# One buffer each for rounded q and its remainder, 24 resident weight tiles, and k's subtraction halved in one block of six, in a fused attention and soft-MoE kernel

## The chip, the cores and the metric

The kernel runs on one core of one Trainium2 chip. The metric is device time in microseconds (us) of one execution.

## The reference

```python
scores = scale * np.matmul(q, k.transpose(0, 1, 3, 2))   # 8 batches, 12 heads, 448 x 64
scores = np.where(causal mask, -1e9, scores)
attn = softmax(scores)
x = (attn @ v) reordered to (3584, 768)                   # rows: tokens, columns: heads
logits = x @ phi                                          # 768 x 32 slots
d = softmax of logits over all 3584 tokens; slot_input = d.T @ x
slot_out[e] = relu(slot_input[e] @ w1[e]) @ w2[e]         # 8 experts, 4 slots each, 768 -> 1024 -> 768
c = softmax of logits over the slots
return c @ slot_out
```

All arrays are float32. The weights w1 and w2 of the eight experts are 50.3 MB together, read once.

## The kernel before, in words

**Two parts.** The first part (about 300 us) is attention, with the logits and slot sums kept up to date behind it. The second (about 100 us) runs the experts and writes the output. The weights come as 64 tiles of 768 KB (`[128, 1536]` f32). `RES` of them are resident: they have a place of their own and are loaded during attention, one every other block. The next `TW1` tiles lie where the buffers of attention lay, so each of their loads waits until the last reader of the buffer under it is done; the rest reuse places of tiles that are used up. `place` and `slot` (lines 144 to 161) say which.

**Attention by pairs.** `block(p)` (lines 536 to 650) runs for each of 48 pairs of heads; pair p has heads a = 2p and a + 1. The engines take their instructions in the order in which the program is written; all of them are recorded by one helper, so every row of the profile has line 65, and one goes by tile names. q and k are split into a rounded value and a remainder, so that the fast matmul gives float32 scores:

- `cast_q`, `cast_k` (ACT, lines 226 to 232) round the raw q into `qd`, the raw k into `ks`. In the profile: `qd<-qk` and `ks<-qk`.
- `sub_k` (POOL, line 234) replaces the lower 64 partitions of `ks` by raw k minus rounded k: `ks<-qk,ks`. `sub_q` (POOL, line 244) writes raw q minus rounded q to the lower half of `r2`: `r<-qk,qd`. One instruction does both heads (64x896), or one head (64x448).
- `copy_k2` (ACT) copies rounded k into `k2`: `k<-ks`.
- `scores1` (PE, line 250) is the first pass, `ks` by `qd`, with the mask: `s<-qd,ks`, `s<-tri,identb`. Its first product of a head, part "k3", takes the last 64 rows of the head and two columns more (`KP`, line 265): the profile shows a weight load of 66 columns. For the first head of a pair those two columns belong to the second head.
- `max_keys`, `max_row` (DVE, PE) find a maximum for every block of 32 queries, giving `mr`. `max_spread` (POOL, line 315) writes it into the upper rows of `r2`: `r<-mr`, called a spread below.
- `scores2` (PE, line 326) is the second pass, `k2` by `r2`: `s<-r,k`. It adds the remainder of q and takes off the maximum. `exps` (ACT) is the exponential, `pt<-s`; `attv_pair` (PE) is `po<-va,pt`; `xtrans` (PE) is `xm<-ident,x`.

Block p finishes pair p (second pass, exponentials, attention times v), does the first pass of pair p + 1, the subtractions `sub_q(p + 1)` and `sub_k(p + 2)`, the casts `cast_q(p + 2)` and `cast_k(p + 3)`, and issues the loads of raw q of pair p + 3 and raw k of pair p + 4 on SP's queue, each behind the subtraction that frees its buffer. `qd`, `r2` and `ks` have two buffers each (`NR = 2`, lines 100 to 108), taken in turn by pairs; the raw values share four (`raw`, line 92).

POOL's work in a block is, in order: `sub_q`, `sub_k`, the spread of head a + 2, the spread of head a + 3. One block in six (p % 6 == 2, p over 6: p = 8, 14, 20, 26, 32, 38, 44) has the softmax step of the logits of a batch as well (`logits_b`, `logits_d`, `logits_e`). Below, "the block of the logits" is such a block, and the text uses p = 32, between 207 and 214 us.

**The start.** `warm(n)` (line 214) puts n matmuls without use on PE, to keep it running; `START` says how many at which place. Pairs 0 and 1 are done head by head.

Of the kernel before, what the change touches and what calls it, by code (L numbers as in the profile page):

```python
# [17 lines left out]
P = 128  # L18
# [7 lines left out]
NCH = 4  # L26
# [4 lines left out]
NEG = -float(2 ** 33)  # L31
NHD = 2 * NPAIR
NR, XB, XT = 2, 3, 2
RES, TW1 = 23, 12

HT = 2
WN, PAD = 1536, 168
WARM = (2, 5, 2, 3, 3)
START = (8, 3, 2)


FILL = 9
# [38 lines left out]
def attention_soft_moe(ctx: ExitStack, tc: tile.TileContext, qk, va, phi, w1, w2, out):  # L81
    nc = _Core(tc)
    const = ctx.enter_context(tc.tile_pool(name="const", bufs=1, side="left"))
    wone = ctx.enter_context(tc.tile_pool(name="wone", bufs=1, side="left"))
# [7 lines left out]
    raw = early.enter_context(tc.tile_pool(name="raw", bufs=4, side="right"))  # L92
# [4 lines left out]


    x_, va_, pt_ = [None] * XB, [None, None], [None, None]
    qd_, ks_ = [fix.tile([P, 2, S], F32R, name="qd0")], [fix.tile([P, 2 * S + KP], F32R, name="ks0")]  # L100
    r2_ = [fix.tile([P, 2, S], F32R, name="r20")]
    qd_.append(fix.tile([P, 2, S], F32R, name="qd1"))
    ks_.append(fix.tile([P, 2 * S + KP], F32R, name="ks1"))
    va_[0] = fix.tile([P, NCH, 2, VC], F32, name="va0")
    x_[1] = fix.tile([P, NCH, 3 * P], F32, name="x1")
    r_ = [fix.tile([P, RW], F32, name=f"r{i}") for i in range(2)]
    k2_ = fix.tile([P, 2 * S + KP], F32R, name="k2")
    r2_.append(fix.tile([P, 2, S], F32R, name="r21"))
    pt_[0] = wk.tile([P, 1024], F32, name="pt0")
    va_[1] = wk.tile([P, NCH, 2, VC], F32, name="va1")  # L110
    pt_[1] = wk.tile([P, 1024], F32, name="pt1")
    ltn = moe.tile([P, P + 1], F32, name="lt")
    lt = ltn[:, 0:P]

    x_[2] = moe.tile([P, NCH, 3 * P], F32, name="x2")
    x_[0] = moe.tile([P, NCH, 3 * P], F32, name="x0")
    gs = moe.tile([P, P], F32, name="gs")
    mk = moe.tile([P, P], F32, name="mk")

    st = {}  # L120

    def load_qk(p, a, hs=slice(0, 2), eng=nc.sync):
        if p < NPAIR:
            if hs.start == 0:

                st["raw", a, p] = (wres.tile([P, 2 * WN], F32, tag="w", name=f"qk{a}_{p}")[:, 0:2 * S]
                                   .rearrange("p (h s) -> p h s", h=2)
                                   if (p, a) in ((1, 0), (2, 1)) else
                                   raw.tile([P, 2, S], F32, tag="qk", name=f"qk{a}_{p}"))
            eng.dma_start(out=st["raw", a, p][:, hs], in_=qk[p, :, a, hs])  # L130

    def loads_v(p, eng=nc.sync):
# [18 lines left out]
    def slot(n, name, dtype=F32):  # L151
        m = place(n)
        if m >= RES:
            return wt[0].tile([P, WN], dtype, tag=f"wa{m}", name=name)
        if m == RES - 1:
            return wone.tile([P, WN], dtype, tag="w1", name=name)
# [41 lines left out]
    for x in (x_[1], x_[0], x_[2]):  # L198
        nc.vector.memset(x[:, NCH - 1], 0.0)
    nc.scalar.activation(out=identb, in_=ident, func=AF.Copy)  # L200
    load_qk(1, 1, eng=nc.scalar)
    load_qk(2, 0)
    load_qk(3, 1)
    for i in range(NR):
        nc.gpsimd.memset(r2_[i][0:64, :, :].bitcast(F32), 0.0)
# [19 lines left out]

    def cast_q(p, hs=slice(0, 2)):
        if p < NPAIR:
            nc.scalar.activation(out=qd_[p % NR][:, hs], in_=st["raw", 0, p][:, hs], func=AF.Copy)

    def cast_k(p, hs=slice(0, 2)):  # L230
        if p < NPAIR:
# [11 lines left out]

    def sub_q(p, hs=slice(0, 2), eng=None):
        if p < NPAIR:
            (eng or nc.gpsimd).tensor_tensor(out=r2_[p % NR][64:P, hs], in0=st["raw", 0, p][64:P, hs],
                                             in1=qd_[p % NR][64:P, hs], op=ALU.subtract)


    def scores1(i, part):  # L250
        if i >= NHD:
            return
        p, h = divmod(i, 2)
        ks, qd = ks_[p % NR], qd_[p % NR]
# [60 lines left out]
    def max_spread(i):  # L315
        if i >= NHD:
            return
        p, h = divmod(i, 2)
        mr = st.pop(("mr", i))

        nc.gpsimd.affine_select(out=r2_[p % NR][0:NQB, h].rearrange("p (b t)->p b t", t=32),
                                in_=mr.unsqueeze(1).to_broadcast([NQB, NQB, 32]),
                                compare_op=ALU.is_equal, fill=0.0, base=0,
                                pattern=[[-1, NQB], [0, 32]], channel_multiplier=1)

    def scores2(i, cs):
        if i >= NHD:
            return
        p, h = divmod(i, 2)
        s = st["s", i]  # L330
        k2, r2 = k2_, r2_[p % NR]
# [187 lines left out]
    cast_k(0, h1)  # L519
    cast_q(0, h1)  # L520
    sub_k(0, h1)
    max_row(0, 0)
    max_row(0, 1)
    max_spread(0)
# [11 lines left out]
    def block(p):  # L536
        a, b = 2 * p, p // 6 - 1
        last, m6 = p == NPAIR - 1, p % 6
        if p + 1 < NPAIR:
            loads_v(p + 1, nc.sync if p + 1 < NPAIR - 1 else nc.scalar)  # L540
        if p % 2 and p // 2 < RES - 1 or p == 2 * RES - 2:
            load_w(p // 2)

        if last:
            for f in last_of:
# [5 lines left out]
        if p == 0:  # L551
            copy_k2(0, h1)
            cast_q(1, h1)
            max_row(1, 0)
# [55 lines left out]
        max_row(a + 2, 1)  # L610
        max_spread(a + 2)
        if p == 0:
            sub_q(1, h1)
            load_qk(3, 0)
        for k in (1, 2):
            max_keys(a + 3, k)
        for k in range(2):
# [350 lines left out]
```

## Time and profile before

| what | value |
|---|---|
| median of 3 runs | 404.52 us (403.7 to 406.21) |
| the profiled execution, device time | 403.89 us |
| its span in the trace | 402.2 us |
| busy: PE, PEld, DVE, ACT, POOL | 368.3, 295.8, 293.7, 282.4, 265.3 us |
| DMA | 119.17 MB, 294 GB/s over the span |
| granted TensorE clock | 0.984 |

In a timeline row the columns are the start, the time of the group, engine, line, operation, written tile <- read tiles, their shapes and the count; in brackets stands the idle time of the engine before it and what ended it. PEld is TensorE's weight load, which runs beside PE. A row of the stretches gives the length, busy time and number of instructions of each engine, the granted clock, the busy share of the DMA engines and what they moved.

### The profile page before, as it was taken

How to read it: one execution, taken by the hardware profiler on the slowest of the kernel's cores; microseconds unless marked ns; L12 is line 12 of the kernel's file. 1: busy time of each engine (PE TensorE's matmuls, PEld its weight loads, DVE VectorE, ACT ScalarE, POOL GpSimd, SP SyncE). 2: the span in 40 equal slices, each digit the busy share in tenths (PEclk: the TensorE clock that was granted, in tenths of full speed). 3: DMA queues.
4: the chain of work that ended last, by engine and by line, in shares of the span. 5: the costliest groups of instructions: out<-in, count | busy, mean ns of one | idle time of the engine just before them, and what ended most of it. 6: DMA issues, size and time to landing. Idle time of an engine off the chain costs nothing.

```text
span 402.2 us, 14066 instructions
## 1 busy us (share of the span) xinstructions
PE 368.3 (92%) x5756; PEld 295.8 (74%) x5756; DVE 293.7 (73%) x834; ACT 282.4 (70%) x395; POOL 265.3 (66%) x214
## 2 busy tenths in 40 slices
PE   6889899999999999999999999999999989997840
PEld 3678888898988898888888889888876544542420
DVE  5868788788898888898888888888975575342540
ACT  5878798898898888888888988988952112432430
POOL 5899899898898988898988989888950000000000
PEclk9999999999999999999999999999999999999985
DMA  8668877878787788777788787788679999999997
GB/s 304 230 199 282 271 266 228 245 279 278 229 286 262 244 269 289 256 240 265 262 270 259 249 272 238 274 286 257 216 279 415 420 420 423 424 418 413 398 397 339
DMA packets 34480, 119.17 MB, mean 296 GB/s; under 512 B 3824, under 2 KB 8944, under 8 KB 32880
## 3 DMA queue, kind: packets, MB, share of 16 engines
q1 hardware_dynamic: 34128, 117.55, 82.2%
q8 instruction: 45, 0.74, 0.7%
q10 hardware_dynamic: 288, 0.73, 0.5%
q14 instruction: 19, 0.16, 0.1%
HBM read 107.25 MB, written 11.01 MB: 294 GB/s over the span
## 4 chain that ended last, share of the span: by engine, by line
PE 54%; DMA 16%; POOL 12%; issue 5%; ACT 4%; DVE 4%; SPq 1%; POOLq 0%; DVEq 0%; ACTq 0%
PE s L65 28%; PE po L65 17%; DMA w<-in_w_dram 14%; POOL r L65 7%; POOL ks L65 5%; PE xm L65 3%; PE rt L65 1%; ACT ks L65 1%; PE pp L65 1%; DVE r L65 1%; DMA qk<-in_qk_dram 1%; PE hp L65 1%; ACT k L65 1%; DVE si L65 1%; PE e L65 1%
## 5 line engine op out<-in xcount | busy, mean ns | idle before, releaser
L65 DVE TRANSPOSE_TENSOR_REDUCE r<-s 128x32 f32<-128x1024 f32 x96 | 119.5, 1245 | 11.4 <-PE s L65 9.3
L65 ACT ACTIVATE pt<-s 128x1024 f32<-128x1024 f32 x96 | 98.8, 1029 | 40.6 <-PE s L65 37.8
L65 PEld LDWEIGHTS po<-va,pt 128*64 128x64 f32 x3040 | 103.6, 138 | 12.0 <-issue 11.9
L65 PE MATMUL po<-va,pt 128*64 128x65 f32 x3040 | 110.6, 224 | 0.0
L65 POOL TENSOR_TENSOR r<-qk,qd 64x896 fp32r<-64x896 f32 (+1 forms) x50 | 101.7, 2033 | 5.5 <-ACT qd L65 1.8
L65 POOL TENSOR_TENSOR ks<-qk,ks 64x896 fp32r<-64x896 f32 (+1 forms) x49 | 99.2, 2024 | 0.2
L65 PE MATMUL s<-qd,ks 128*128 128x448 f32 (+4 forms) x384 | 80.8, 322 | 0.6 <-POOL ks L65 0.4
L65 POOL TENSOR_SCALAR_AFFINE_SELECT r<-mr 14x448 fp32r<-14x448 f32 x96 | 61.5, 643 | 29.8 <-PE xm L65 18.6
L65 PE MATMUL s<-r,k 128*128 128x448 f32 (+3 forms) x384 | 65.2, 292 | 5.0 <-POOL r L65 4.3
L65 PEld LDWEIGHTS s<-r,k 128*128 128x128 f32 (+1 forms) x384 | 59.3, 176 | 11.0 <-POOL r L65 8.8
L65 PEld LDWEIGHTS s<-qd,ks 128*128 128x128 f32 (+2 forms) x384 | 52.8, 184 | 3.7 <-issue 1.4
L65 ACT ACTIVATE qd<-qk 128x896 fp32r<-128x896 f32 (+1 forms) x50 | 46.0, 920 | 1.7 <-DMA qk<-in_qk_dram 0.8
L65 ACT ACTIVATE k<-ks 64x896 fp32r<-64x896 f32 (+1 forms) x49 | 45.8, 934 | 1.2
L65 ACT ACTIVATE ks<-qk 128x896 fp32r<-128x896 f32 (+1 forms) x51 | 45.4, 892 | 1.1 <-DMA qk<-in_qk_dram 1.0
L65 PE MATMUL s<-tri,identb 128*128 128x192 bf16 x192 | 39.4, 270 | 1.1 <-DVE si L65 0.4
L65 DVE TENSOR_REDUCE r<-r 128x16 f32<-128x32 f32 x192 | 33.7, 176 | 5.0
L65 DVE TENSOR_REDUCE mr<-s 14x32 f32<-14x128 f32 x47 | 13.1, 279 | 23.1 <-ACT ks L65 12.8
L65 PE MATMUL xm<-ident,x 128*128 128x128 f32 x188 | 28.3, 273 | 0.0
L65 ACT ACTIVATE xts<-xm 128x512 f32<-128x512 f32 x47 | 27.8, 592 | 0.2 <-PE xm L65 0.2
L65 DVE TENSOR_SCALAR x<-po,sm 64x64 f32<-64x64 f32 x94 | 25.9, 276 | 0.7
L65 DVE TENSOR_TENSOR x<-po,sm 128x384 f32<-128x384 f32 (+2 forms) x49 | 25.7, 526 | 0.0
L65 DVE COPY ot<-pp 128x384 f32<-128x384 f32 x26 | 13.6, 554 | 13.4 <-PE pp L65 13.3
(138 smaller groups left out, 391.0 us busy)
## 6 DMA issues: line engine op xcount, KB each, us to landing
qk<-in_qk_dram SPq DMA_DIRECT2D x93, 448.0 KB, 4.4
w<-in_w_dram SPq DMA_DIRECT2D x43, 768.0 KB, 7.0
w<-in_w_dram SPq DMA_DIRECT2D x10, 1536.0 KB, 21.0
va<-in_va_dram SPq DMA_DIRECT2D x47, 260.0 KB, 4.6
out_dram<-ot SPq DMA_DIRECT2D x16, 384.0 KB, 6.7
out_dram<-ot SPq DMA_DIRECT2D x2, 1536.0 KB, 9.2
qk<-in_qk_dram SPq DMA_DIRECT2D x4, 224.0 KB, 3.9
hw<-in_w_dram SPq DMA_DIRECT2D x1, 768.0 KB, 8.4
```

Of the source, the lines that this page charges most:

```text
L65: return self._tc.keep_in_program_order(op(*args, **kwargs))
```

## The change

It has five parts.

1. `qd` and `r2` get one buffer each. So `cast_q(p + 2)` in block p has to follow `sub_q(p + 1)`, which reads `qd`; and `sub_q(p + 1)` has to follow the second passes of pair p, which read `r2`.
2. In a block, `sub_k(p + 2)` now stands ahead of `sub_q(p + 1)`, and `cast_k(p + 3)` ahead of `cast_q(p + 2)`. The loads behind them change places in the same way. Raw k and raw q have two buffers each instead of four together.
3. In the block of the logits, and in block 1, `sub_k` is halved: the first head's half stands ahead of `sub_q`, the second head's half behind both spreads, and the load of raw k of pair p + 4 behind that.
4. `RES` goes from 23 to 24 and `TW1` from 12 to 11. Two more blocks (16 and 30) load a tile, block 44 none. All resident tiles now lie in pairs. The buffers of attention are placed in another order, which changes which reader a later load waits for.
5. At the start, raw k of pair 1 is loaded by SP instead of ACT's queue, behind the loads of pair 0; raw k of pair 3 is loaded after `sub_k(0)`; the subtractions of pairs 1 to 3 stand in another order; one of two memsets of `r2` goes; `START` is (9, 6, 2, 4) in place of (8, 3, 2): one, three and four more warming matmuls, the last group at a new place.

The diff without the renaming of buffers:

```diff
-RES, TW1 = 23, 12
+RES, TW1 = 24, 11
-START = (8, 3, 2)
+START = (9, 6, 2, 4)
...
-    qd_, ks_ = [fix.tile([P, 2, S], F32R, name="qd0")], [fix.tile([P, 2 * S + KP], F32R, name="ks0")]
-    r2_ = [fix.tile([P, 2, S], F32R, name="r20")]
-    qd_.append(fix.tile([P, 2, S], F32R, name="qd1"))
+    kraw = {n: fix.tile([P, 2, S], F32, name=f"kraw{n}") for n in (0, 1)}
+    qraw = {0: fix.tile([P, 2, S], F32, name="qraw0")}
+    ks_ = [fix.tile([P, 2 * S + KP], F32R, name="ks0")]
+    qd = fix.tile([P, 2, S], F32R, name="qd")
     ks_.append(fix.tile([P, 2 * S + KP], F32R, name="ks1"))
+    qraw[1] = fix.tile([P, 2, S], F32, name="qraw1")
...
-    r2_.append(fix.tile([P, 2, S], F32R, name="r21"))
+    r2 = fix.tile([P, 2, S], F32R, name="r2")
...
-            if n <= NBUF or q >= RES - 1:
+            if n <= NBUF or q >= RES:
...
     for hs in (slice(0, 1), slice(1, 2)):
         load_qk(0, 1, hs)
         load_qk(0, 0, hs)
+    load_qk(1, 1)
     load_qk(1, 0)
...
-    load_qk(1, 1, eng=nc.scalar)
     load_qk(2, 0)
-    load_qk(3, 1)
+    nc.gpsimd.memset(r2[0:64, :, :].bitcast(F32), 0.0)
...
-        if p % 2 and p // 2 < RES - 1 or p == 2 * RES - 2:
-            load_w(p // 2)
+        if p % 2 and p < 44 or p in (16, 30):
+            load_w(st["w"])
+            st["w"] += 1
...
-        if p:
+        late_k = p == 1 or m6 == 2 and p > 6
+        if p == 1:
+            sub_q(2, h0)
+            sub_k(3, h0)
+            sub_q(2, h1)
+            load_qk(4, 0)
+        elif p:
+            sub_k(p + 2, h0 if late_k else slice(0, 2))
+            if not late_k:
+                load_qk(p + 4, 1)
             sub_q(p + 1)
             load_qk(p + 3, 0)
-            sub_k(p + 2)
-            load_qk(p + 4, 1)
         else:
             sub_q(1, h0)
+            sub_q(1, h1)
+            load_qk(3, 0)
             sub_k(2, h0)
...
-        cast_q(p + 2)
-        cast_k(p + 3)
+        if p:
+            cast_k(p + 3)
+            cast_q(p + 2)
...
         max_spread(a + 3)
-        if p == 0:
-            sub_k(2, h1)
-            load_qk(4, 1)
+        if late_k:
+            sub_k(p + 2, h1)
+            load_qk(p + 4, 1)
```

POOL in blocks 32 (of the logits) and 33, before; `mr66` and `mr67` are the spreads at the end of block 32, `qk0` is raw q and `qk1` raw k, with the pair behind it:

```order
L65 TENSOR_TENSOR r21_98<-qk0_33_3261,qd1_91 64x896
L65 TENSOR_TENSOR ks0_89<-qk1_34_3264,ks0_89 64x896
L65 AFFINE_SELECT r21_98<-mr66_3505 14x448
L65 AFFINE_SELECT r21_98<-mr67_3516 14x448
L65 TENSOR_TENSOR r20_90<-qk0_34_3359,qd0_88 64x896
L65 TENSOR_TENSOR ks1_92<-qk1_35_3362,ks1_92 64x896
L65 AFFINE_SELECT r20_90<-mr68_3605 14x448
```

And with the change, where `kraw` and `qraw` are the raw values:

```order
L65 TENSOR_TENSOR ks0_85<-kraw0_82,ks0_85 64x448
L65 TENSOR_TENSOR r2_94<-qraw1_88,qd_86 64x896
L65 AFFINE_SELECT r2_94<-mr66_3445 14x448
L65 AFFINE_SELECT r2_94<-mr67_3456 14x448
L65 TENSOR_TENSOR ks0_85<-kraw0_82,ks0_85 64x448
L65 TENSOR_TENSOR ks1_87<-kraw1_83,ks1_87 64x896
L65 TENSOR_TENSOR r2_94<-qraw0_84,qd_86 64x896
L65 AFFINE_SELECT r2_94<-mr68_3545 14x448
```

Half of the subtraction of `ks0` (pair 34) has moved behind the two spreads, ahead of the work of block 33.

PE at the start of block 33, with the semaphores for which a row waits, before: the second pass of head 66 (`r21`, `k2`), then the first pass of head 68 into `s2`:

```order
L65 MATMUL s0_85<-r21_98,k2_97 128x448 [waits Pool_49]
L65 MATMUL s0_85<-r21_98,k2_97 128x320
L65 MATMUL s0_85<-r21_98,k2_97 128x192
L65 MATMUL s0_85<-r21_98,k2_97 66x64
L65 LDWEIGHTS identb_132
L65 MATMUL s2_87<-tri2_123,identb_132 128x192 [waits DVE_49]
L65 MATMUL s2_87<-qd0_88,ks0_89 66x64 [waits Activation_49]
```

And with the change:

```order
L65 MATMUL s0_79<-r2_94,k2_93 128x448 [waits Pool_49]
L65 MATMUL s0_79<-r2_94,k2_93 128x320
L65 MATMUL s0_79<-r2_94,k2_93 128x192
L65 MATMUL s0_79<-r2_94,k2_93 66x64
L65 LDWEIGHTS identb_127
L65 MATMUL s2_81<-tri2_118,identb_127 128x192 [waits DVE_49]
L65 MATMUL s2_81<-qd_86,ks0_85 66x64 [waits Activation_49,Pool_49]
```

PE's order is the same; the first product of the first pass (66x64) waits for POOL as well. The instruction of POOL for which it waits is the second half of `ks0` in the rows above.

SP's queue at the end of attention, before, with the loads of the first tiles that lie on buffers of attention (`w23` on):

```order
L65 DMA va0_93<-in_va_dram 128x520 [waits DMAHW2_49,DMAHW1_49,PE_49]
L65 DMA w23_5154<-in_w2_dram 128x1536 [waits DMAHW4_49,DMAHW5_49,DMAHW3_49,Pool_49]
L65 DMA w24_5156<-in_w1_dram 128x1536 [waits DMAHW0_49,Pool_49]
L65 DMA w25_5158<-in_w1_dram 128x1536 [waits PE_49]
L65 DMA w26_5160<-in_w1_dram 128x1536 [waits DMAHW6_49,PE_49]
L65 DMA w27_5162<-in_w1_dram 128x1536 [waits DMAHW7_49,Activation_49]
```

And with the change:

```order
L65 DMA va0_89<-in_va_dram 128x520 [waits DMAHW4_49,DMAHW2_49,PE_49]
L65 DMA w24_5072<-in_w1_dram 128x1536 [waits DMAHW6_49,Pool_49]
L65 DMA w25_5074<-in_w1_dram 128x1536 [waits DMAHW5_49,PE_49,DMAHW7_49,Activation_49,Pool_49]
L65 DMA w26_5076<-in_w1_dram 128x1536 [waits PE_49,Activation_49,Pool_49]
L65 DMA w27_5078<-in_w1_dram 128x1536 [waits DMAHW1_49]
```

Of POOL's instructions, `w23` before waits for `sub_k(47)` and `w24` for `sub_q(47)`; with the change `w24` waits for `sub_k(47)` of block 45, `w25` for `sub_q(46)` of the same block, and `w26` for `sub_q(47)` of block 46.

More of the change, by code (lines that the diff above doesn't have):

```diff
@@ L83, in attention_soft_moe @@
     const = ctx.enter_context(tc.tile_pool(name="const", bufs=1, side="left"))
-    wone = ctx.enter_context(tc.tile_pool(name="wone", bufs=1, side="left"))
     wres = ctx.enter_context(tc.tile_pool(name="wres", bufs=RES // 2, side="left"))
@@ L91, in attention_soft_moe @@
     fix = early.enter_context(tc.tile_pool(name="fix", bufs=1, side="right"))
-    raw = early.enter_context(tc.tile_pool(name="raw", bufs=4, side="right"))
     ps_1 = att.enter_context(tc.tile_pool(name="ps_1", bufs=1, space=PSUM))
@@ L99, in attention_soft_moe @@
     x_, va_, pt_ = [None] * XB, [None, None], [None, None]
-    qd_, ks_ = [fix.tile([P, 2, S], F32R, name="qd0")], [fix.tile([P, 2 * S + KP], F32R, name="ks0")]
-    r2_ = [fix.tile([P, 2, S], F32R, name="r20")]
-    qd_.append(fix.tile([P, 2, S], F32R, name="qd1"))
+    kraw = {n: fix.tile([P, 2, S], F32, name=f"kraw{n}") for n in (0, 1)}
+    qraw = {0: fix.tile([P, 2, S], F32, name="qraw0")}
+    ks_ = [fix.tile([P, 2 * S + KP], F32R, name="ks0")]
+    qd = fix.tile([P, 2, S], F32R, name="qd")
     ks_.append(fix.tile([P, 2 * S + KP], F32R, name="ks1"))
+    qraw[1] = fix.tile([P, 2, S], F32, name="qraw1")
     va_[0] = fix.tile([P, NCH, 2, VC], F32, name="va0")
+    r_ = [fix.tile([P, RW], F32, name=f"r{i}") for i in range(2)]
     x_[1] = fix.tile([P, NCH, 3 * P], F32, name="x1")
-    r_ = [fix.tile([P, RW], F32, name=f"r{i}") for i in range(2)]
     k2_ = fix.tile([P, 2 * S + KP], F32R, name="k2")
-    r2_.append(fix.tile([P, 2, S], F32R, name="r21"))
+    r2 = fix.tile([P, 2, S], F32R, name="r2")
     pt_[0] = wk.tile([P, 1024], F32, name="pt0")
+    pt_[1] = wk.tile([P, 1024], F32, name="pt1")
     va_[1] = wk.tile([P, NCH, 2, VC], F32, name="va1")
-    pt_[1] = wk.tile([P, 1024], F32, name="pt1")
+    x_[2] = moe.tile([P, NCH, 3 * P], F32, name="x2")
+    x_[0] = moe.tile([P, NCH, 3 * P], F32, name="x0")
     ltn = moe.tile([P, P + 1], F32, name="lt")
     lt = ltn[:, 0:P]
-    x_[2] = moe.tile([P, NCH, 3 * P], F32, name="x2")
-    x_[0] = moe.tile([P, NCH, 3 * P], F32, name="x0")
     gs = moe.tile([P, P], F32, name="gs")
     mk = moe.tile([P, P], F32, name="mk")
-    st = {}
+    st = {"w": 0}
     def load_qk(p, a, hs=slice(0, 2), eng=nc.sync):
@@ L128, in load_qk @@
                                    if (p, a) in ((1, 0), (2, 1)) else
-                                   raw.tile([P, 2, S], F32, tag="qk", name=f"qk{a}_{p}"))
+                                   kraw[p % 2 if p > 1 else 1 - p] if a else qraw[p % 2 if p else 1])
             eng.dma_start(out=st["raw", a, p][:, hs], in_=qk[p, :, a, hs])
@@ L227, in cast_q @@
         if p < NPAIR:
-            nc.scalar.activation(out=qd_[p % NR][:, hs], in_=st["raw", 0, p][:, hs], func=AF.Copy)
+            nc.scalar.activation(out=qd[:, hs], in_=st["raw", 0, p][:, hs], func=AF.Copy)
     def cast_k(p, hs=slice(0, 2)):
@@ L245, in sub_q @@
         if p < NPAIR:
-            (eng or nc.gpsimd).tensor_tensor(out=r2_[p % NR][64:P, hs], in0=st["raw", 0, p][64:P, hs],
-                                             in1=qd_[p % NR][64:P, hs], op=ALU.subtract)
+            (eng or nc.gpsimd).tensor_tensor(out=r2[64:P, hs], in0=st["raw", 0, p][64:P, hs],
+                                             in1=qd[64:P, hs], op=ALU.subtract)
     def scores1(i, part):
@@ L253, in scores1 @@
         p, h = divmod(i, 2)
[L254 removed]
+        ks = ks_[p % NR]
         if ("s", i) not in st:
@@ L330, in scores2 @@
         s = st["s", i]
-        k2, r2 = k2_, r2_[p % NR]
+        k2 = k2_
         for c in cs:
@@ L521, in attention_soft_moe @@
     sub_k(0, h1)
+    load_qk(3, 1)
     max_row(0, 0)
@@ L553, in block @@
             cast_q(1, h1)
+            warm(START[3], pob)
             max_row(1, 0)
@@ L587, in block @@
             logits_d(b, lt)
-        cast_q(p + 2)
-        cast_k(p + 3)
+        if p:
+            cast_k(p + 3)
+            cast_q(p + 2)
+        else:
+            cast_q(2)
+            cast_k(3)
         if m6 == 3 and p > 6:
@@ L612, in block @@
         if p == 0:
-            sub_q(1, h1)
-            load_qk(3, 0)
+            sub_k(2, h1)
+            load_qk(4, 1)
         for k in (1, 2):
```

5 lines of the change are left out of this document (1 added, 4 removed).

## The prediction

> **What bounds the kernel now.** I read the page's slices first, then one block of the logits and the block after it instruction by instruction (32 and 33), then the end.
>
> ```profile
> PE   6889899999999999999999999999999989997840
> POOL 5899899898898988898988989888950000000000
> DMA  8668877878787788777788787788679999999997
> ```
>
> Up to slice 30 (about 300 us) PE is nearly always busy, POOL almost as much, and DMA has room. From then on DMA is full and POOL has nothing to do. So attention is bound by PE with POOL close behind, the end by DMA. How close shows around block 32. POOL first, then PE's weight loads:
>
> ```profile
> 208.66 2.12 POOL L65 TENSOR_TENSOR r<-qk,qd 64x896 fp32r<-64x896 f32 x1
> 210.72 2.12 POOL L65 TENSOR_TENSOR ks<-qk,ks 64x896 fp32r<-64x896 f32 x1
> 212.91 1.24 POOL L65 TENSOR_SCALAR_AFFINE_SELECT r<-mr 14x448 fp32r<-14x448 f32 x2
> 214.24 2.12 POOL L65 TENSOR_TENSOR r<-qk,qd 64x896 fp32r<-64x896 f32 x1
> 216.31 2.12 POOL L65 TENSOR_TENSOR ks<-qk,ks 64x896 fp32r<-64x896 f32 x1
> 218.49 0.64 POOL L65 TENSOR_SCALAR_AFFINE_SELECT r<-mr 14x448 fp32r<-14x448 f32 x1
> ```
>
> ```profile
> 212.66 0.47 PEld L65 LDWEIGHTS xm<-ident,x 128*128 128x128 f32 x4
> 213.60 0.60 PEld L65 LDWEIGHTS s<-r,k 128*128 128x128 f32 x4 [0.47 <-POOL r L65]
> 214.18 0.15 PEld L65 LDWEIGHTS s<-qd,ks 128*66 128x66 f32 x1
> 219.30 0.47 PEld L65 LDWEIGHTS xm<-ident,x 128*128 128x128 f32 x4
> 219.74 0.61 PEld L65 LDWEIGHTS s<-r,k 128*128 128x128 f32 x4
> 220.50 0.14 PEld L65 LDWEIGHTS s<-qd,ks 128*66 128x66 f32 x1
> ```
>
> At 213.60 PE had waited 0.47 us for the first of the two spreads: here POOL is the bound. One block later the spread ends at 218.49 + 0.64 = 219.13, and PE takes up the second pass at 219.74, straight behind its transposes (219.30 + 0.47 = 219.77): PE is the bound, and POOL has 0.6 us to spare. The next five blocks leave PE no gap in which time could be won back (29.16 us busy of 29.26):
>
> ```profile
> 219.74:249.00 29.26, 29.16 (x502) 25.76 (x501) 25.44 (x70) 25.23 (x34) 26.35 (x19) 1.00 0.79 258
> ```
>
> **The halved subtraction, seven blocks.** In block 32 POOL will run half of sub_k, sub_q, spread, spread, the other half. The maxima that the spreads need, and a half by itself (two from the start, so the step from one to the next shows too):
>
> ```profile
> 212.01 0.24 DVE L65 TENSOR_REDUCE mr<-rt 14x32 f32<-14x128 f32 x1
> 213.07 0.28 DVE L65 TENSOR_REDUCE mr<-s 14x32 f32<-14x128 f32 x1 [0.18 <-PE s L65]
> 10.09 1.14 POOL L65 TENSOR_TENSOR ks<-qk,ks 64x448 fp32r<-64x448 f32 x1
> 11.19 1.14 POOL L65 TENSOR_TENSOR r<-qk,qd 64x448 fp32r<-64x448 f32 x1
> ```
>
> What it removes: sub_q ends at 208.66 + 1.10 + 2.12 = 211.88 instead of 212.84, the first spread can start when its maximum is there, 212.01 + 0.24 = 212.25, and ends by 212.95. PE then goes on at 212.66 + 0.47 = 213.13 and not at 213.60: 0.47 us won.
>
> What it adds: the second spread can't be earlier than its maximum, 213.07 + 0.28 = 213.35. It ends at 213.35 + 0.06 + 0.64 = 214.05. The late half follows 0.09 behind (as 214.24 follows 214.15), takes 1.13, and ends at 215.27. The first matmul of the first pass loads 66 columns of ks, two of them from the second head, and in the order of instructions it now waits for POOL. So it starts at 215.27 + 0.07 = 215.34 (the 0.07 as from spread to PE: 212.91 + 0.62 = 213.53 to 213.60). It stood at 214.18. The 0.47 us won is spent waiting here, and 1.16 us more is lost: **+1.16 us** a block. Behind it on PE wait the rest of the first pass, the second pass of the other head, and all that follows, since PE runs in order. POOL is no second loss: its next spread ends at 214.05 + 0.09 + 1.10 + 2.07 + 2.18 + 0.64 = 220.13, before PE comes for it at 219.74 + 1.16 = 220.90.
>
> The late half also frees raw k later. In block 33 ACT rounds k first, then q:
>
> ```profile
> 218.67 0.93 ACT L65 ACTIVATE ks<-qk 128x896 fp32r<-128x896 f32 x1
> 219.51 0.28 ACT L65 ACTIVATE al<-run_m,run_m 128x1 f32<-128x1 f32 x1
> qk<-in_qk_dram SPq DMA_DIRECT2D x1, 448.0 KB, 3.6
> qk<-in_qk_dram SPq DMA_DIRECT2D x1, 448.0 KB, 4.1
> ```
>
> The load is issued at 215.3. Loads from the same place in earlier blocks landed in 3.6 to 4.1 us, so by 219.4; the cast of k takes 0.84 (218.67 to 219.51), that of q 0.95: ready at 221.2 at the latest, and PE wants it at 220.50 + 1.16 = 221.66. Hidden; it would show from a landing time of 4.5 us.
>
> The ends: 0.46 us if only the second head waited for the late half (then POOL's 220.13 + 0.07 against 219.74 decides), 1.63 if the 0.47 were not won either. I take 1.16, which both rows and order give. Six of the seven blocks make 7.0 us; the seventh (44) reaches into the end and is counted there.
>
> **The single buffers in the other blocks.** sub_q and sub_k change places, so their sum on POOL stays at 2.07 + 2.18. The cast of q follows the pair: in block 32's rows 212.84 + 0.06 + 0.95 = 213.85, and PE wants it at 214.18: hidden by the spread and the second pass, with 0.26 us left after the 0.07. sub_q waits for the second pass of the other head, which is over while sub_k runs. I take 0. If a block were short by 0.1 us more than the margin, 39 blocks would give 3.9 us.
>
> **The end.** These stretches, and what starts the loads:
>
> ```profile
> 296.00:298.00 2.00, 2.00 (x60) 1.85 (x60) 1.72 (x5) 1.33 (x3) 0.27 (x1) 1.00 0.56 129
> 298.00:300.00 2.00, 2.00 (x25) 1.19 (x15) 0.94 (x5) 0.00 (x0) 0.73 (x2) 1.00 1.00 397
> 320.00:330.00 10.00, 9.54 (x165) 4.99 (x158) 7.78 (x32) 1.24 (x4) 0.00 (x0) 1.00 1.02 427
> PE so L65 <- DMA w<-in_w_dram: 3.7, 5, 1.0
> 291.33 0.33 SPq L65 DMA_DIRECT2D w<-in_w_dram  x1
> 295.79 0.33 SPq L65 DMA_DIRECT2D w<-in_w_dram  x1
> 293.66 2.11 POOL L65 TENSOR_TENSOR r<-qk,qd 64x896 fp32r<-64x896 f32 x1
> 294.07 0.62 PE L65 MATMUL s<-r,k 128*128 128x448 f32 x4
> ```
>
> One tile (w23, issued at 291.33) goes into idle DMA time. The next, w24, issued at 295.79 when sub_q(47) is over (293.66 + 2.11 = 295.77), starts a stream that doesn't break: 40 tiles, 0.786 MB each, 1.84 us at 427 GB/s. With the change w23 is resident, and w24 and w25 go into the idle time, behind sub_k(47) and sub_q(46). The stream starts with w26: 38 tiles, 3.7 us less. But w26 waits for sub_q(47), which with a single r2 waits for the second pass of head 93: it ended at 294.07 + 0.62 = 294.69, now 1.16 later at 295.85. So sub_q(47) ends at 298.0, and the stream starts 298.1 - 295.79 = 2.3 us later. Net **-1.4 us**, block 44's share in it. PE can follow: it waits 3.7 us for tiles there, and needs 1.4 + 1.16 = 2.6. The ends: -2.6 if block 44's share isn't there, +1.2 if the tiles bring nothing.
>
> **The start.**
>
> ```profile
> 16.41 0.64 POOL L65 TENSOR_SCALAR_AFFINE_SELECT r<-mr 14x448 fp32r<-14x448 f32 x1 [0.76 <-DVE mr L65]
> 25.68 0.15 PEld L65 LDWEIGHTS s<-qd,ks 128*66 128x66 f32 x1
> 4.75 0.58 ACT L65 ACTIVATE qd<-qk 128x448 fp32r<-128x448 f32 x1 [0.75 <-DMA qk<-in_qk_dram]
> ```
>
> POOL's 0.76 us wait is filled with work, but the late half of pair 3 is again what the first pass waits for at 25.68, and POOL does the same sum in smaller pieces: about 0. The warming matmuls fill waits of PE. ACT waits 0.75 us for q's first half; with pair 1's k behind it this can shrink. I take -0.2, between -0.8 and +0.6. The Trainium skill's page "DMA: Bandwidth & Descriptors", section "Issuing engines are not separate DMA queues", says that transfers from different engines share the same DMA engines and interleave. By it the load taken off ACT's queue did slow q's first half, and I would put -0.4 here, 409.1 in all; no row here tells the two loads apart.
>
> **Sum**, from the profiled execution's own 403.89 us (402.2 of it span; the median of the runs is 0.63 above): 403.89 + 7.0 - 1.4 - 0.2 = **409.3 us**, 5.4 us or 1.3% slower.
>
> **The rivals.**
>
> A, on the other side: the late half costs only what POOL is late. If the first matmul didn't wait for the second head's half, or PE won the time back, a block costs 0.46: 403.89 + 6 x 0.46 - 2.1 - 0.2 = 404.4 us, not slower (at the end 0.7 us more is won than above, since block 44's share shrinks by it). It decides if the first pass starts before POOL's late half ends. For it: two columns of 66 are all that is needed. Against: the order shows the wait, and PE has no gap. Chance 0.17.
>
> B, faster: the 0.47 us won is kept, at 0.4 in seven blocks, and the end gives 2.6: 403.89 - 2.8 - 2.6 - 0.2 = 398.3 us. The late half would have to be over by 213.7; its maximum comes at 213.35. Chance 0.05.
>
> C, slower still: the single qd and r2 make ordinary blocks wait. At 0.1 us past the margin, 409.3 + 3.9 = 413.2 us. Against it stands the 0.26 us. Chance 0.1. The Trainium skill, page "Trainium Kernel Development and Optimization", section "Best Practices", asks for double buffers so that work overlaps; by that rule C is the likely case. The rows show what covers the wait, and I go by them.
>
> D: the end gives nothing, because PE or the places of used tiles hold the stream: 403.89 + 7.0 + 1.2 - 0.2 = 411.9 us. Chance 0.1.
>
> **The numbers.** My forecast has 0.58. The range is 404.0 to 412.5 us: A's time below, D and most of C above. The median is 404.52 us, and about 1% is what a measurement of this kernel can tell from no change, so 400.5 and 408.6 are the bounds. Slower: most of the forecast, C and D, 0.64. Faster: B and a little of A, 0.07. The same: 0.29.
>
> **What would show it.** Right: a wait of PE for POOL's ks of about 1.6 us at the first pass of blocks 9, 15, 21, 27, 33, 39 and 45; no wait for r there any more; these blocks' periods 1.2 us longer in all; DMA full from about 2 us later relative to attention's end, and some 2.6 us less between the last pass of attention and the end. Wrong: first passes that start before the late half ends (A), waits of PE for qd in ordinary blocks (C), or more idle DMA time after 300 us (D).

## The result and the profile after

| | before | after |
|---|---|---|
| median | 404.49 us (4 runs, 403.7 to 406.21) | 410.47 us (4 runs, 409.64 to 410.99) |
| ratio | | 1.014, 95% interval 1.0103 to 1.0177 |
| the profiled execution, its span | 403.89, 402.2 us | 410.65, 408.9 us |
| transposes of block 7 begin | 60.59 us | 60.29 us |
| from there to the transposes of block 46 | 238.29 us | 246.16 us |
| from the transposes of block 47 to the end | 100.14 us | 99.27 us |

The change made the kernel 1.4% slower. The three last lines divide the span into the start, the blocks and the end. They are read from PE's weight loads `xm<-ident,x`, which end every block (block 47's stand at 302.06 before and 309.63 after). First the rows of before:

```profile
60.59 0.47 PEld L65 LDWEIGHTS xm<-ident,x 128*128 128x128 f32 x4
298.88 0.47 PEld L65 LDWEIGHTS xm<-ident,x 128*128 128x128 f32 x4
```

And of after:

```profile
60.29 0.47 PEld L65 LDWEIGHTS xm<-ident,x 128*128 128x128 f32 x4
306.45 0.47 PEld L65 LDWEIGHTS xm<-ident,x 128*128 128x128 f32 x4
```

So 0.30 us were won at the start, 7.87 us lost in the blocks and 0.87 us won at the end: 6.70 us in all, which is the difference of the spans. Where in the blocks? Read at blocks 9, 15, 21, 27, 33, 39 and 45, after stands 0.86, 2.01, 3.15, 4.31, 5.25, 6.40 and 7.56 us behind before. Each of the seven logits blocks costs 0.94 to 1.16 us, and the blocks between them nothing: blocks 21 to 26, for instance, end 3.15 us behind, as they began. (Only between blocks 27 and 32 do 0.10 us move the other way, which is why the smallest of the seven reads 0.94.)

POOL in blocks 32 and 33, after:

```profile
212.86 1.15 POOL L65 TENSOR_TENSOR ks<-kraw,ks 64x448 fp32r<-64x448 f32 x1
213.98 2.10 POOL L65 TENSOR_TENSOR r<-qraw,qd 64x896 fp32r<-64x896 f32 x1
216.53 0.64 POOL L65 TENSOR_SCALAR_AFFINE_SELECT r<-mr 14x448 fp32r<-14x448 f32 x1 [0.45 <-DVE mr L65]
217.63 0.64 POOL L65 TENSOR_SCALAR_AFFINE_SELECT r<-mr 14x448 fp32r<-14x448 f32 x1 [0.46 <-DVE mr L65]
218.35 3.19 POOL L65 TENSOR_TENSOR ks<-kraw,ks 64x448 fp32r<-64x448 f32 x2
221.49 2.11 POOL L65 TENSOR_TENSOR r<-qraw,qd 64x896 fp32r<-64x896 f32 x1
223.68 0.64 POOL L65 TENSOR_SCALAR_AFFINE_SELECT r<-mr 14x448 fp32r<-14x448 f32 x1
```

PE's weight loads at the same place:

```profile
216.87 0.47 PEld L65 LDWEIGHTS xm<-ident,x 128*128 128x128 f32 x4
217.31 0.60 PEld L65 LDWEIGHTS s<-r,k 128*128 128x128 f32 x4
219.52 0.13 PEld L65 LDWEIGHTS s<-qd,ks 128*66 128x66 f32 x1 [1.54 <-POOL ks L65]
```

The first spread is in time now: PE takes up the second pass at 217.31 without a wait. POOL stands idle for 0.45 and 0.46 us, waiting for the two maxima, and only then runs the late half (the first part of the row at 218.35). It ends at about 219.46, and PE's load of 66 columns of ks starts at 219.52, after 1.54 us of idle time. The waits of PE's weight loads between 60 and 290 us (in total, how often, the longest), before and then after:

```profile
PEld s L65 <- POOL r L65: 2.6, 7, 0.5
```

```profile
PEld s L65 <- POOL ks L65: 9.3, 6, 1.6
```

The wait for r is gone, and one for ks has come in its place: about 1.55 us a time instead of 0.37. Six of the seven lie in that stretch; the last, 1.54 us long, ends at 294.71.

### The profile page after: what moved, and what is told of

Read it like the earlier page. It is cut to its first block, busy times and chain, and to the rows that moved or that the text cites. A ratio compares the mean times of both kernels' runs of the same rounds, so it can differ in the third digit from the quotient of the medians.

```text
span 408.9 us, 14057 instructions
## 1 busy us (share of the span) xinstructions
PE 368.8 (90%) x5764; PEld 296.5 (73%) x5764; DVE 293.7 (72%) x834; ACT 286.1 (70%) x395; POOL 265.8 (65%) x222
## 5 line engine op out<-in xcount | busy, mean ns | idle before, releaser
L65 POOL TENSOR_TENSOR r<-qraw,qd 64x896 fp32r<-64x896 f32 (+1 forms) x49 | 99.2, 2024 | 3.0 <-ACT qd L65 1.7
L65 POOL TENSOR_TENSOR ks<-kraw,ks 64x896 fp32r<-64x896 f32 (+1 forms) x55 | 98.2, 1791 | 4.4 <-ACT ks L65 0.8
L65 ACT ACTIVATE ks<-kraw 128x896 fp32r<-128x896 f32 (+1 forms) x49 | 44.9, 918 | 5.0 <-DMA kraw<-in_qk_dram 3.5
L65 ACT ACTIVATE qd<-qraw 128x896 fp32r<-128x896 f32 (+1 forms) x48 | 44.7, 931 | 3.6 <-POOL r L65 1.7
L65 PE MATMUL s<-tri,identb 128*128 128x192 bf16 x192 | 40.4, 270 | 1.1 <-DVE si L65 0.4
L65 PEld LDWEIGHTS <-identb 128*128 128x128 bf16 x219 | 21.1, 98 | 2.4 <-issue 1.4
```

Source lines behind the costliest of these rows:

```text
L65: return self._tc.keep_in_program_order(op(*args, **kwargs))
```

## The experiments

All times are medians; a ratio is to the kernel before, run on the same chip. The three columns of the profile are those of the table above; each is one execution.

| kernel | time, us | ratio (95%) | block 7 | 7 to 46 | 47 to end |
|---|---|---|---|---|---|
| before | 404.49 | 1 | 60.59 | 238.29 | 100.14 |
| after | 410.47 | 1.014 (1.0103 to 1.0177) | 60.29 | 246.16 | 99.27 |
| sub_k whole | 402.23 | 0.9925 (0.9899 to 0.995) | 59.95 | 238.14 | 98.93 |
| first product of 64 | 407.78 | 1.0066 (1.0046 to 1.0087) | 59.78 | 244.44 | 99.50 |
| before with the late half | 413.82 | 1.0231 (1.0188 to 1.0274) | 60.26 | 246.37 | 101.19 |
| half between the spreads | 405.03 | 1.000 (0.9976 to 1.0025) | 59.91 | 240.59 | 99.22 |
| half on DVE | 405.05 | 1.0006 (0.9988 to 1.0023) | 60.13 | 240.56 | 99.82 |
| after again | 411.05 | 1.0159 (1.0133 to 1.0185) | 60.41 | 246.59 | 99.11 |
| after, load in the gap | 411.14 | 1.0164 (1.0138 to 1.019) | 60.22 | 246.19 | 99.80 |
| after, load in the stream | 412.66 | 1.0198 (1.0173 to 1.0223) | 59.89 | 246.20 | 101.73 |
| before again | one profile | | 61.86 | 238.27 | 100.58 |

### The late half: taken out, and put in alone

The first kernel is the changed one with k's subtraction whole everywhere but in block 1:

```diff
-        late_k = p == 1 or m6 == 2 and p > 6
+        late_k = p == 1
```

> The changed kernel (410.5 us) with k's subtraction whole and ahead of q's in the blocks of the logits too; single buffers, 24 resident tiles and the start stay. If the late half is what costs (my theory: 1.16 us in each of seven blocks by the prediction; the second spreads after blocks 8 to 44 show 1.12 to 1.16 each, 7.9 us in all), the time is 402.5 us, 0.5% under the kernel before. If the late half were only where the time shows and the single buffers or the other order of the subtractions made these blocks longer (rival), the time stays near 410.5 us, with a wait of PE for r in place of that for ks. If the single buffers cost 0.1 us in ordinary blocks, it is 406.4 us.

Measured: 402.23 us, faster than the kernel before. The blocks take 238.14 us, 0.15 less than before the change, and PE waits for r again where it waited before:

```profile
PEld s L65 <- POOL r L65: 2.6, 7, 0.4
```

The second is the kernel before with nothing but the late half:

```diff
-            sub_k(p + 2)
-            load_qk(p + 4, 1)
+            late_k = m6 == 2 and p > 6
+            sub_k(p + 2, h0 if late_k else slice(0, 2))
+            if not late_k:
+                load_qk(p + 4, 1)
...
+        elif m6 == 2 and p > 6:
+            sub_k(p + 2, h1)
+            load_qk(p + 4, 1)
```

> The kernel before (404.5 us) with one thing of the change: in the blocks of the logits sub_k is halved, the second head's half behind both spreads, and the load of raw k behind that. Double buffers, 23 resident tiles and the old start stay. If the half by itself costs 1.14 us in each of seven blocks, the time is 404.5 + 8.0 = 412.5 us (ratio 1.020). If it needs the single buffers to do harm (rival), it is 404.5 us.

Measured: 413.82 us. The blocks take 246.37 us, 8.08 more than before, with the same wait as after the change:

```profile
PEld s L65 <- POOL ks L65: 9.3, 6, 1.6
```

Taken together, the late half is the whole loss in the blocks. With it the loss is there under double buffers too; without it the single buffers and the other order of the subtractions, taken together, cost nothing in any block.

### What the wait itself costs, and what stands behind it

This kernel leaves the late half where the change put it, but PE's first product doesn't need it:

```diff
-min(P, S - P * c + (KP if i > 4 or i % 2 else 0))
+min(P, S - P * c + (KP if i % 2 or i > 4 and (p % 6 != 4 or p < 10) else 0))
```

> The changed kernel with the late half in its place, but the first product of the first head of the pairs 10, 16, ..., 46 takes 64 columns of k instead of 66, in both passes, so that it needs nothing of the second head's half. The two rows of scores that are left out belong to no key of that head. If PE's wait for the late half is the cause, 0.46 us a block stay (POOL, late with the next spread, decides then): 410.5 - 7 x 0.68 = 405.7 us, and PE's wait for ks gives way to one of 0.9 us for r. If the time is lost because POOL has more to do behind the spreads (rival), nothing is won: 410.5 us. If PE has slack later, 402.5 us.

Measured: 407.78 us, 2 us more than expected. The blocks take 244.44 us, so a logits block still costs 6.15 / 7 = 0.88 us and not 0.46. PE's waits between 60 and 290 us, for its weight loads:

```profile
PEld s L65 <- POOL r L65: 3.3, 6, 0.6
PEld s L65 <- ACT qd L65: 1.9, 7, 0.7
...
PEld s L65 <- POOL ks L65: 0.6, 3, 0.3
```

POOL is late with r, as expected, by about 0.55 us a time. In and behind block 33, PE's weight loads that waited:

```profile
218.37 0.13 PEld L65 LDWEIGHTS s<-qd,ks 128*66 128x66 f32 x1 [0.27 <-POOL ks L65]
223.20 0.60 PEld L65 LDWEIGHTS s<-r,k 128*128 128x128 f32 x4 [0.55 <-POOL r L65]
224.41 0.14 PEld L65 LDWEIGHTS s<-qd,ks 128*66 128x66 f32 x1 [0.53 <-ACT al L65]
```

The first two are POOL's lateness. For the third, the expectation had forgotten the second thing that the late half holds up, the load of raw k behind it. In this kernel's block 33 it is issued on SP at 218.34, and ACT has to wait for it; ACT's queue there:

```profile
222.00 0.95 ACT L65 ACTIVATE ks<-kraw 128x896 fp32r<-128x896 f32 x1 [1.69 <-DMA kraw<-in_qk_dram]
222.86 0.93 ACT L65 ACTIVATE qd<-qraw 128x896 fp32r<-128x896 f32 x1
223.70 0.28 ACT L65 ACTIVATE al<-run_m,run_m 128x1 f32<-128x1 f32 x1
```

q's cast follows k's, and `al`, a factor of the logits' softmax, follows both. At this place the last wait of the chain is not PE's for qd, which is there by 223.79, but goes over `al` and DVE: DVE's `si<-si,al,s` has waited 0.94 us for `al` when it starts at 224.01. It reads the tile `s`, and PE's next first pass waits for it. It ends at 224.36, and PE starts at 224.41, 0.53 us late. PE's waits of this kind, in the list of its matmuls between 60 and 290 us, were 0.4 us in one place before the change, and are here:

```profile
PE s L65 <- DVE si L65: 1.9, 6, 0.5
```

Around block 33 the three waits, less the 0.47 us that PE waited in their place before the change, make the whole loss: 0.27 + 0.55 + 0.53 - 0.47 = 0.88. So of the 1.12 us that a logits block costs on average after the change (7.87 / 7), taking away the wait for the 66 columns wins only 0.25. The lateness of POOL and of the load, until then hidden under that wait, decides.

### The half at another place

Here the second half runs as soon as the first spread is done:

```diff
-        if p == 0:
+        if p == 0 or late_k and p > 1:
             sub_k(p + 2, h1)
             load_qk(p + 4, 1)
         for k in (1, 2):
...
-        if late_k:
+        if p == 1:
             sub_k(p + 2, h1)
```

> The changed kernel with the second head's half between the two spreads instead of behind them. POOL waited 0.45 us there for the second maximum. By the durations in the trace, the first spread ends, the half takes 1.12 us more, and PE's first product can start 5.5 us after the first half began, as it did before the change; the second spread ends 0.6 us later than before, which is what POOL had to spare. So if only the place of the half matters: 402.5 us, like the whole subtraction. If halving itself costs (a second instruction, a later load of raw k): 403 to 405 us. If the second spread then comes too late for PE (rival), 0.3 us or more a block: 404.6 us or more.

Measured: 405.03 us, the time of the kernel before and 2.8 us more than with sub_k whole; the rival has it. The blocks take 240.59 us, 0.33 more per logits block than before the change. POOL, in this kernel's block 32:

```profile
210.51 2.09 POOL L65 TENSOR_TENSOR r<-qraw,qd 64x896 fp32r<-64x896 f32 x1
213.07 0.64 POOL L65 TENSOR_SCALAR_AFFINE_SELECT r<-mr 14x448 fp32r<-14x448 f32 x1 [0.46 <-DVE mr L65]
213.79 1.14 POOL L65 TENSOR_TENSOR ks<-kraw,ks 64x448 fp32r<-64x448 f32 x1
215.00 0.64 POOL L65 TENSOR_SCALAR_AFFINE_SELECT r<-mr 14x448 fp32r<-14x448 f32 x1
```

PE's weight loads beside it:

```profile
214.98 0.13 PEld L65 LDWEIGHTS s<-qd,ks 128*66 128x66 f32 x1 [0.47 <-POOL ks L65]
215.69 0.60 PEld L65 LDWEIGHTS s<-r,k 128*128 128x128 f32 x4 [0.20 <-POOL r L65]
```

POOL still idles 0.46 us for the first maximum, with the half that could fill it standing behind. That idle time comes back as a wait of 0.47 us for ks, which takes the place of the 0.47 for the first spread before the change, and one of 0.20 for r, which is new. In the undivided order POOL had no idle time there at all. The rest of the 0.33 us falls at the next pair's first pass: ACT's cast of q (at 219.91) waits 0.41 us for sub_q, because qd has one buffer, and `al`, `si` and PE's first product (at 221.50) follow, as in the experiment before. Here, then, the single buffer is no longer covered.

### Work taken off POOL

If POOL's sum of work is what bounds a logits block, the half could go to DVE:

```diff
-            sub_k(p + 2, h1)
+            sub_k(p + 2, h1, nc.vector if p else None)
```

(at the place of the experiment before).

> The kernel with sub_k whole (402.2 us), but in the blocks of the logits the second head's half runs on DVE, behind the first maximum of the block, and so is off POOL. There PE waited 0.37 to 0.47 us in each of seven blocks for POOL's first spread. If POOL's sum of work is what bounds these blocks, up to 7 x 0.47 = 3.3 us are won: 399 us. Rival: DVE, which is busy without a gap from there to the second maximum, passes the half's 0.5 us on to the first maximum of the next block, and nothing is won: 402 us or more.

Measured: 405.05 us, 2.8 us more than with sub_k whole (by medians taken beside two different measurements of the kernel before, 404.36 and 405.21): nothing is won, as the rival says. The list of the waits of PE's weight loads between 60 and 290 us has none for POOL any more, but this one:

```profile
PEld s L65 <- DVE r L65: 5.3, 7, 0.8
```

DVE and POOL in this kernel's block 32, DVE first:

```profile
212.48 0.24 DVE L65 TENSOR_REDUCE mr<-rt 14x32 f32<-14x128 f32 x1
212.74 0.62 DVE L65 TENSOR_TENSOR ks<-kraw,ks 64x448 fp32r<-64x448 f32 x1
213.40 0.40 DVE L65 TENSOR_REDUCE r<-r 128x16 f32<-128x32 f32 x2
```

```profile
212.79 1.08 POOL L65 TENSOR_SCALAR_AFFINE_SELECT r<-mr 14x448 fp32r<-14x448 f32 x1 [0.50 <-DVE mr L65]
214.64 0.64 POOL L65 TENSOR_SCALAR_AFFINE_SELECT r<-mr 14x448 fp32r<-14x448 f32 x1 [0.77 <-DVE mr L65]
```

The half takes 0.62 us on DVE, against 1.14 on POOL, but it stands ahead of the reductions that PE's next transpose needs (at 213.85, after 0.75 us of waiting). So DVE passes the half on to PE in the same block, and not, as the rival had it, to a maximum of the next one. The seven waits make 5.3 us, where those for r made 2.6 with sub_k whole; the blocks are 2.4 us longer (240.56 against 238.14). And the spread that ran beside it took 1.08 us instead of 0.64, in all seven logits blocks (1.08 or 1.09). The Trainium skill, page "SBUF — State Buffer", section "SBUF: two separate sides", says that a DVE instruction with two inputs from SBUF and a GpSimd instruction that reads SBUF share one pair of ports, and that the later of the two waits for the whole of the other. The trace agrees that the spread is held up: the subtraction has two such inputs and started 0.05 us ahead of the spread. The size fits less well, since the spread's excess is 0.44 us and the rest of the subtraction was 0.57 (0.62 - 0.05). PE did not wait for this spread.

### The end: is the stream of tiles the bound all along?

The prediction had put the end at -2.6 us relative to the last pass of attention; the profiles show -0.87. The changed kernel's DMA share and GB/s (the last two columns) in the stretch in question, and then those of before at the same distance from block 47:

```profile
312.00:314.00 2.00, 1.38 (x31) 1.03 (x26) 1.58 (x9) 0.19 (x1) 0.00 (x0) 1.00 0.96 377
314.00:315.00 1.00, 1.00 (x22) 0.71 (x21) 0.42 (x1) 0.19 (x1) 0.00 (x0) 1.00 0.86 147
315.00:316.00 1.00, 1.00 (x18) 0.49 (x6) 0.29 (x1) 0.35 (x2) 0.00 (x0) 1.00 0.82 301
316.00:317.00 1.00, 0.88 (x16) 0.45 (x17) 0.70 (x4) 0.51 (x4) 0.00 (x0) 1.00 0.94 344
```

```profile
304.50:306.50 2.00, 1.37 (x27) 1.03 (x24) 1.54 (x8) 0.26 (x1) 0.00 (x0) 1.00 1.04 421
306.50:307.50 1.00, 1.00 (x22) 0.64 (x20) 0.42 (x1) 0.12 (x1) 0.00 (x0) 1.00 0.99 399
307.50:308.50 1.00, 0.95 (x14) 0.49 (x7) 0.29 (x1) 0.42 (x2) 0.00 (x0) 1.00 1.04 430
308.50:309.50 1.00, 0.93 (x15) 0.52 (x19) 0.77 (x4) 0.51 (x3) 0.00 (x0) 1.00 0.95 393
```

After the change the stream has a gap at 314 to 317 us: by these rates it moves about 1.1 us' worth less than before. The stream begins with four tiles, w26 to w29, where six stood before; w30 and the tiles behind it wait for the end of attention. SP's queue at the issue of w30, before and then after:

```profile
304.18 3.94 SPq L65 DMA_DIRECT2D w<-in_w_dram  x3
```

```profile
311.69 4.00 SPq L65 DMA_DIRECT2D w<-in_w_dram  x3
```

It comes 7.51 us later, as attention's end does (7.57). Two kernels fill or don't fill that gap with one tile that is loaded twice, and the changed kernel runs beside them:

```diff
     for n in range(RES, NBUF):
         load_w(n)
+        if n == 29:
+            nc.sync.dma_start(out=wtiles[order[24]], in_=w1[4, 0][:, 0:WN])
```

and, in the other, in the loop of the later loads:

```diff
             load_w(n)
+            if n == 40:
+                nc.sync.dma_start(out=wtiles[order[24]], in_=w1[4, 0][:, 0:WN])
             n += 1
```

> The changed kernel once more, unaltered, as the measure for the two runs with one more load, and for how much the start and the end of the same program differ between two profiled executions. From the last transposes of attention (block 47) to the end, the changed kernel took 99.27 us; three other kernels with the same 24 resident tiles took 98.93 to 99.50; the kernel before took 100.14. Theory: about 99.3 us again, 410.5 us in all.

> The changed kernel with one tile (w24, 0.786 MB) loaded a second time into its own place, issued between w29 and w30, just ahead of the stretch where the DMA engines ran short of work (0.90, 0.74 and 0.97 busy, 184, 233 and 332 GB/s in three successive microseconds, about 1.1 us of lost transfer). Theory: the shortage took part of the end's gain, so the extra load fills it first and costs only 1.84 - 1.1 = 0.7 us more than the changed kernel. Rival: the stream is the bound throughout, and the load costs 1.8 us. Second rival: the end is bound by PE, and it costs 0.

> The changed kernel with the same tile loaded a second time, but 10 us later, between w38 and w40, where the DMA engines are full. Theory: 1.84 us more than the changed kernel (0.786 MB at 427 GB/s), 1.1 us more than the extra load in the gap. If the end is bound by PE there: 0.

Measured: 411.05, 411.14 and 412.66 us. In the gap the load costs 0.1 us, in the stream 1.6 us. DMA share and GB/s of the kernel with the load in the gap:

```profile
314.00:315.00 1.00, 1.00 (x22) 0.67 (x20) 0.42 (x1) 0.16 (x1) 0.00 (x0) 1.00 1.00 412
315.00:316.00 1.00, 0.98 (x15) 0.49 (x6) 0.29 (x1) 0.39 (x2) 0.00 (x0) 1.00 1.02 424
316.00:317.00 1.00, 0.90 (x15) 0.48 (x19) 0.73 (x4) 0.51 (x3) 0.00 (x0) 1.00 1.00 418
```

So the gap took some 1.5 us of the end's gain (412.66 - 411.14). That the load costs 1.6 us in the stream speaks against PE as the bound of the end. The size is rough: six runs of one of these kernels spread over 1.2 to 2.3 us, the ends of the three profiles (99.11, 99.80 and 101.73 us) give 0.7 and 2.6 us for the two loads, and 0.7 and 1.8 were expected. By a single profile the end differs by up to about 0.5 us between executions of one program, so the kernel before was profiled again:

> The kernel before once more, unaltered, as the measure for start and end. From the last transposes of attention (block 47) to the end it took 100.14 us in the one profile so far, and block 7 reached its transposes at 60.59 us. Theory: 100 to 100.5 us and 60.3 to 60.6; the six kernels with 24 resident tiles took 98.93 to 99.82 there, and 59.78 to 60.41 for the start. If the end falls under 99.8 us, the change's end has won nothing that a profile can show.

Its end took 100.58 us. The kernel before, again, and with the late half: 100.14, 100.58 and 101.19, 100.64 in the mean. After, again, sub_k whole, first product of 64, half between, and half on DVE: 98.93 to 99.82, 99.31 in the mean. The three kernels of the next section, also with 24 resident tiles, lie in that range (98.93, 99.67 and 99.67). The end's gain is 1.3 us; the gap's 1.5 us added would make 2.8, and 2.6 were predicted. That is a sum of two rough numbers: no kernel was run with the stream of the change and no gap.

### The start

> The kernel with sub_k whole (402.2 us), with the load of raw k of pair 1 back on ACT's queue, as before the change. If that load took bandwidth from q's first half, as the page on descriptors of the Trainium skill would have it, ACT rounds q's first half 0.4 us later and block 7 comes 0.4 us later (60.3 instead of 59.95). If the two loads do not meet there (my theory, from the traces so far, in which ACT rounds q's first half at 4.65 to 4.75 us with the load on its queue): the same within 0.2 us.

> The same with the old counts of warming matmuls too (8, 3 and 2, and none at the new place). If the warming brings something at the start, block 7 comes later than in the run with the load on ACT's queue alone; theory: within 0.3 us of it, since these matmuls only fill waits of PE.

> The kernel with sub_k whole, with the load of raw k of pair 1 on ACT's queue again, this time issued as early as in the kernel before (at about 1.4 us, between SP's loads of pair 0). In three profiles with that load there (the kernel before twice, the late half alone), ACT rounded q's first half at 4.65 to 5.49 us, after a wait of 0.69 to 1.52 us for it; in eight profiles with the load on SP's queue behind pair 0, at 3.85 to 4.06 us with no wait. If that load takes bandwidth from q's first half, as the page on descriptors of the Trainium skill has it, the wait is back: 4.6 us or later. If another part of the change at the start brought it: 3.9 to 4.1 us and no wait.

The edits, all to the kernel with sub_k whole (the second changes `START` alone, so the load of pair 1's raw k stays on SP's queue in it, and it is read beside the kernel with sub_k whole):

```diff
-    load_qk(1, 1)
     load_qk(1, 0)
...
+    load_qk(1, 1, eng=nc.scalar)
```

```diff
-START = (9, 6, 2, 4)
+START = (8, 3, 2, 0)
```

```diff
-    load_qk(1, 1)
+    load_qk(1, 1, eng=nc.scalar)
     load_qk(1, 0)
```

In the first the load on ACT's queue went out at 3.52 us only, not at 1.41 as in the kernel before. So it says nothing on q's first half; it shows what a late k of pair 1 costs: ACT had it at 11.24 us, and block 7 came at 62.43. In the second block 7 came at 60.53, against 59.78 to 60.41 in eight profiles with the new counts: the warming may bring a few tenths, within what executions differ by. With the load at 1.41 us on ACT's queue, ACT waited 0.69 to 1.52 us for q's first half in all three profiles; with it on SP's queue behind pair 0, in none of nine. In the third kernel it went out at 0.80 us, not at 1.41, and so ahead of most of pair 0's loads. ACT's queue there:

```profile
0.80 0.41 ACTq L65 DMA_DIRECT2D kraw<-in_qk_dram  x1
...
5.17 0.58 ACT L65 ACTIVATE ks<-kraw 128x448 fp32r<-128x448 f32 x1 [2.32 <-DMA kraw<-in_qk_dram]
5.92 0.58 ACT L65 ACTIVATE qd<-qraw 128x448 fp32r<-128x448 f32 x1 [0.18 <-DMA qraw<-in_qk_dram]
```

And after the change, with the load on SP's queue:

```profile
3.29 0.58 ACT L65 ACTIVATE ks<-kraw 128x448 fp32r<-128x448 f32 x1 [0.88 <-DMA kraw<-in_qk_dram]
3.85 0.58 ACT L65 ACTIVATE qd<-qraw 128x448 fp32r<-128x448 f32 x1
```

An early load on ACT's queue delays pair 0's k and q, k's cast by 1.9 us here, and block 7 comes at 62.35. How much of that is the load's is open: it is one profile, and two profiles of the kernel before have block 7 at 60.59 and 61.86. By the rule of the Trainium skill that the prediction cites (page "DMA: Bandwidth & Descriptors", section "Issuing engines are not separate DMA queues") transfers of both queues interleave on the same DMA engines, and this trace agrees.

## Why the prediction was right, and where it wasn't

**The halved subtraction** was predicted right in place, mechanism and size: 1.16 us in each of seven logits blocks; measured 0.94 to 1.16, 7.87 us in all against 7 x 1.16 = 8.12. PE's wait for ks was to be about 1.6 us and is up to 1.6. The kernel before with the half alone, and the changed kernel without it, show that it is the cause.

**The single buffers** were costed at nothing, with 0.26 us of cover, and cost nothing: 238.14 us from block 7 to 46 with sub_k whole, against 238.29. Rival C falls. The cover is thin, as the half between the spreads shows, where ACT's cast of q waited for sub_q. What the prediction quotes for C from the Trainium skill (page "Trainium Kernel Development and Optimization", section "Best Practices") speaks of overlapping DMA with compute. Both of these buffers are filled by compute engines, so these runs say nothing on it.

**The end** is the step that was mis-sized, though the measure lies between the ends given for it: -1.4 us were predicted with block 44's share. That share, 1.16 us by the prediction's own figure, taken off the sum, leaves -2.6 between attention and the end; measured are -0.87 in the two profiles compared and -1.3 over nine. The start of the stream was right: w26 goes out at 304.53 us, 1.17 us later relative to block 47's transposes than w24 before, and 2.3 - 1.16 = 1.14 were predicted. What failed is the 3.7 us for two tiles. "A stream that doesn't break" was true of the kernel before, and was carried over to the kernel after without a look at what feeds it. With two tiles less at its head and w30 released no earlier, it ran short of work. The issue of w30 and its neighbours, which wait for the end of attention, was in the trace of before and would have told it.

**The start** was put at -0.2 us. The compared profiles have -0.30; three profiles with the old start have block 7 at 60.26 to 61.86 and eight with the new one at 59.78 to 60.41, so the gain may be larger, and no profile alone tells its size. The sentence on the load on ACT's queue, which would have made it -0.4, was nearer to these. How much of the rest belongs to the warming matmuls stays open.

**Rival A** was wrong by the experiment that removed the wait: a block costs 0.88 us and not 0.46. In the block read above POOL's lateness makes 0.35 of it (0.27 + 0.55 - 0.47), and the load of raw k 0.53. That load, "hidden" in the prediction because PE itself came later, is not hidden once PE comes earlier. That condition was in the prediction's sum (its cover was 221.66, and 1.16 of that was the loss itself), and the rival's price left it out. The sum also stopped at q's cast, ready at 221.2, and left out `al` and `si` between the casts and PE; after the change that made no difference.

**Rivals B and D.** B asked that the 0.47 us stay won: they are spent in the wait of 1.54 us for ks. D asked that the end give nothing; it gave 0.9 to 1.3 us of the forecast's 2.6, a third to a half of the way from D to it.

**Sum** in the profiled execution: 403.89 + 7.87 - 0.87 - 0.30 = 410.59, and 410.65 was measured. The forecast of 409.3 is short of this by the end's 1.7 us, less the 0.25 by which the blocks and the 0.1 by which the start came out cheaper, and the rounding.

The version to keep is the changed kernel with sub_k whole in the logits blocks: 402.23 us, ratio 0.9925 (0.9899 to 0.995) to the kernel before.

## What to carry to other kernels

When an instruction is split so that its first part comes earlier, look at who reads the last element of the second part: here two columns of 66 made PE wait for all of it. A cost that hides under a loss is a cost of the next version, so price a repair with everything that the late instruction holds up, its loads too. And a saving in a stream of transfers counts only as long as the stream has something to move: count the tiles that are released, and when, before you multiply tiles by their time.

## What the runs showed of the hardware

A spread on POOL took 1.08 us in place of 0.64 while DVE subtracted two tensors (above). The same tile's load cost 0.1 us or 1.6 by the medians, by its place in the stream, about ten tiles apart. And with one load of 448 KB on a second queue, 0.80 us after the start, k's first cast came at 5.17 us and block 7 at 62.35, against 3.43 and 59.95 with the same load behind the others, though its bytes were the same and were needed anyway; this is one profile of each.
